# Lightning attention and a routed mixture of experts: rows of twelve attention steps turned on VectorE and written in groups of four, six steps with 128-key scores

## The chip, the cores and the metric

The kernel runs on one core of one Trainium2 chip. The time is device microseconds of one execution of the whole program; the result is compared as the median of several runs. Profiled executions are single executions, with their own time.

## The reference

The work has two parts, one feeding the other. First, linear attention with a decay: 4 sequences, 8 heads, 768 positions, head size 64, in float32.

```
for each block of positions:
    intra = (q_b @ k_b.T * lam**(i-j) for i >= j) @ v_b
    inter = (q_b * lam**(i+1)) @ kv_state
    out[block] = intra + inter
    kv_state = lam**block * kv_state + (k_b * lam**(block-1-j)).T @ v_b
x = out with the heads side by side      # 3072 tokens of 512 numbers
```

Then each token goes to one of 8 experts. The gate is `argmax(x @ w_gate)`, unless a local gate (`x @ w_local`) says that the token keeps the expert of the token before it in its sequence. The output of a token is its chosen expert's probability times `relu(x @ w1[e]) @ w2[e]`, with 1024 hidden units. All of it is float32.

## The kernel before

**Attention.** A chunk is 128 positions of one sequence; there are 24 steps `s`, ordered by chunk and within it by sequence (`ORDER`, so s%4 is the sequence b and s//4 the chunk c). One DMA brings the queries, keys and values of a step into a tile `inp` (1 MB, 0.75 MB in the last chunk); six such tiles exist (`LOADS`), so the load of step s+5 (`loaded`, L170) waits until step s-1 has done with its tile. GpSimd prepares three steps ahead: `qd` (L177, queries times powers of lambda) and `kd` (L180, keys times powers). Then, for a step:

- `scores` (L200 or L208): keys by queries into two PSUM tiles `ps`. A step in `WIDE` takes 128 keys at once, 8 matmuls of 128x128 (L200). Another takes 16 matmuls of 64 keys, where half of them skip the queries that lie before their keys (L208). VectorE multiplies the result by the decay mask into `sm` (L212). The same two PSUM tiles serve every step but step 1.
- `from_state` (L235): `qd` by the running state `kv` into `po`; ScalarE then scales the state (L239).
- `mix` (L248): values by `sm`, added in `po`; ScalarE copies it into `xc` (L251), features by tokens, one place for each sequence.
- `update` (L262): `kd` by values into `pk`, which VectorE adds to `kv` (L265; L267 in the first chunk).
- `rows_of(s-1)` (L272): four TensorE transposes of `xc` against the identity into PSUM, a ScalarE copy to `xn` (L277), and a DMA that writes the 128 token rows to `x_dram` (L281). The DMA is issued from ScalarE's queue, for the last steps from SyncE's (SP).

After each chunk, `gates` (L286) computes the gate sums of the four sequences and `logits` (L294, L295) turns them, at the next two steps. The table `extras` places the routing work (constants, the choice of experts, ranks, tables of tokens) at steps 6 to 22 on VectorE mostly: `constants_2` to `constants_6` hold casts of iota tables and of the identity matrix into other types (L333 to L353), `fresh_experts` is L389 to L403, `along_sequences` L411 to L420, `experts_of` L427 to L429, `ranks` L438 to L457.

**Order.** The attention loop writes out the order of the instructions for TensorE, VectorE, SyncE and GpSimd by hand; ScalarE's order is left to the scheduler. From step 5 on, the scores of step s+1 are issued at the start of step s; in steps 1 to 4 they follow `mix(s)`.

**Experts.** The tokens are gathered from `x_dram` by indirect DMA into tiles of 128 rows (L703), turned (L712, or VectorE's 32x32 transpose L717 with ScalarE copies L724), multiplied by the expert's weights (L731 and L737 for one tile at a time, L956 and L961 for two), scaled, and scattered to the output (L746). The weights lie in buffers `w1t` and `w2t` (2 MB each, two of each and a third from the expert stage on). Expert 0 is loaded at steps 16 to 20, expert 1 into `w1t[1]` and `w2t[1]` at the last step. Until then `w1t[1]` is unused, and `w2t[1]` holds start-up tables.

Of the kernel before, what the change touches and what calls it, by code (L numbers as in the profile page):

```python
# [8 lines left out]
F32 = mybir.dt.float32  # L9
# [14 lines left out]
P = 128  # L24
B, H, S, DH = 4, 8, 768, 64
A = H // 2
DM = H * DH
E, F = 8, 1024
DT, FT = DM // P, F // P
N = B * S  # L30
NT = N // P
NC = S // P
# [6 lines left out]
PARTS = [(0, 8), (8, NA), (NA, NT)]  # L39
LOADS = 6  # L40
QUARTERS = [16, 17, 18, 19]
WIDE = [3, 4, 5]
WARM = 10
KA = -(-(NA * P - E * (P - 1)) // P)

# [2 lines left out]
HP = P // 2  # L48
QP = P // 4
# [5 lines left out]
G = G2 + E  # L55
# [9 lines left out]
def kernel(  # L65
# [9 lines left out]
    nc = tc.nc  # L75
# [7 lines left out]
    x_dram = dram.tile([N, DM], F32, name="x_dram")  # L83
# [5 lines left out]
    w1t = [wts.tile([P, DT, F], F32, name=f"w1_{i}") for i in range(2)]  # L89
# [12 lines left out]
    ident = const.tile([P, P], F32, name="ident")  # L102
# [6 lines left out]
    load = x_ctx.enter_context(tc.tile_pool(name="load", bufs=LOADS))  # L109
# [54 lines left out]
    xc = att.tile([P, A, B, P], F32, name="xc", bufs=1)  # L164
    inp, qds, kds, sms, lgs = {}, {}, {}, {}, {}
# [103 lines left out]
    def rows_of(s):  # L269
        px = pg.tile([P, DM], F32, name="pk1")  # L270
        for a in range(A):
            nc.tensor.transpose(px[:, P * a:P * a + P], xc[:, a, ORDER[s][0]], ident)  # L272
        if s + 1 < NS:
            xn = att.tile([P, DM], F32, name="xn", bufs=4)
        else:
            xn = xlast
        nc.scalar.copy(xn, px)  # L277


        queue = nc.scalar if s + 3 < NS else nc.sync  # L280
        queue.dma_start(out=x_dram[P * s:P * s + P, :], in_=xn)  # L281

    def gates(k):

# [18 lines left out]
    count = const.tile([P, G + 1], F32, name="count")  # L303
    countb = const.tile([P, P], BF16, name="countb")
    whole = const.tile([P, G + 1], F32, name="whole")
# [24 lines left out]
            nc.gpsimd.memset(t[:, :, 0:1], 0.0)  # L330

    def constants_2():
        nc.vector.tensor_copy(count, ints[0][:, :G + 1])  # L333
        nc.vector.tensor_copy(whole, ints[0][:, P:P + G + 1])
        nc.vector.tensor_copy(identb, ident)
        nc.vector.tensor_scalar(down, count[:, :E], -1.0, float(E), ALU.mult, ALU.add)

    def constants_3():
        nc.vector.tensor_copy(countb, ints[0][:, :P])

    def constants_4():
        nc.vector.tensor_copy(beforeb, ints[1][:, P:2 * P].bitcast(F32))
        nc.vector.tensor_copy(parts[:, :, 0], whole[:, 1:NT + 1])
        nc.vector.tensor_copy(parts[:, :, 1], ints[0][:, 2 * P:2 * P + NT])

    def constants_5():
        for half in range(2):
            nc.vector.tensor_copy(dupb[:, HP * half:HP * half + HP], ident[:, :HP])
        nc.vector.tensor_reduce(upper, ident[:, HP:], axis=AX.X, op=ALU.add)

    def constants_6():
        for k in range(4):
            nc.vector.tensor_copy(dupq[:, QP * k:QP * k + QP], ident[:, :QP])  # L353
        row = ints[0][:, 2 * P:2 * P + 1]
        nc.vector.tensor_scalar(row, row, P - QP, None, ALU.bitwise_and)
        nc.vector.tensor_scalar(fourth, row, 1.0 / QP, None, ALU.mult)
# [424 lines left out]
    def extra_work(s, k):  # L781
        if (s, k) in extras:
            extras[s, k]()

    with tc.manual_schedule(engines={PE, DVE, SP, POOL}):

        warm = pg.tile([P, A, P], F32, name="pk0")
        for _ in range(WARM):
            nc.tensor.matmul(warm[:, 0], lhsT=ident, rhs=ident, start=True, stop=True)
        masks_of_lam()  # L790
        nc.gpsimd.memset(wgt, 0.0)
        constants_1()

        for s in range(LOADS - 1):
            inp[s] = load.tile([P, 4, DM], F32, name="inp")
        for s, half in ((0, 0), (1, 0), (0, 1), (1, 1), *((s, half) for s in range(2, LOADS - 1) for half in range(2))):
            nc.sync.dma_start(out=inp[s][:, 2 * half:2 * half + 2], in_=qkv[s][:, 2 * half:2 * half + 2])
        for s in range(3):
            prepare(s)
        scores(0)  # L800
        nc.sync.dma_start(out=wgt[:, :, :E + 1], in_=wg)
        for s in range(NS):
            if s + LOADS - 1 < NS:
                loaded(s + LOADS - 1)
            if s + 3 < NS and s != 1:
                prepare(s + 3)
            if s in QUARTERS:
                j = QUARTERS.index(s)
                nc.sync.dma_start(out=w1t[0][:, j], in_=w1_src(0)[:, j])
            if s == NS - 4:  # L810
                nc.sync.dma_start(out=w2t[0], in_=w2_src(0))
                weights(0)
            if s == NS - 1:
                nc.sync.dma_start(out=w1t[1], in_=w1_src(1))
                nc.sync.dma_start(out=w2t[1], in_=w2_src(1))
            if s + 1 < NS and s not in (1, 2, 3, 4, 5):
                scores(s + 1)
            from_state(s)
            if s % B == 1 and s > B:
                logits(s // B - 1)  # L820
            if s == 5:
                scores(6)
            extra_work(s, 0)
            if s % B == 0 and s:
                gates(s // B - 1)
            mix(s)
            if s == 0:
                update(0)
                query_powers(0)
            if s in (1, 2, 3, 4):  # L830
                scores(s + 1)
            if s == 1:
                query_powers(1)
                prepare(4)
                rows_of(0)
            if s:
                update(s)
            if s + 1 == NS:
                first_turned()
            if s > 1:  # L840
                rows_of(s - 1)
            extra_work(s, 1)
        x_ctx.close()
        act = ctx.enter_context(tc.tile_pool(name="act", bufs=2))
        w1t.append(act.tile([P, DT, F], F32, name="w1_2", bufs=1))
        w2t.append(act.tile([P, FT, DM], F32, name="w2_2", bufs=1))
        pools.append(act)

        pys.extend(pg.tile([P, DM], F32, name=f"pk{i}") for i in range(2))
        hq.update({(f, 1): act.tile([P, FT // 2, P], F32, name=f"h{f}1", bufs=1) for f in range(2)})  # L850
        xgh = act.tile([P, DM], F32, name="xgh", bufs=1)
        yt = act.tile([P, 2, DM], F32, name="y", bufs=1)
        xps = [act.tile([P, DT, P], F32, name=f"xp{i}", bufs=1) for i in range(3)]
        xs = act.tile([P, 3, DT // 2, P], F32, name="xs", bufs=1)
        s1 = act.tile([P, 3, DT // 2, F // 2], F32, name="s1", bufs=1)
        yl = s1[:, 0]
        s2 = act.tile([P, 3, FT // 2, DM // 2], F32, name="s2", bufs=1)
        hs = act.tile([P, 4, FT // 2, P], F32, name="hsum", bufs=1)
        part = act.tile([P, 3, FT // 2, P], F32, name="part", bufs=1)
        rest = act.tile([P, DM // 2], F32, name="rest", bufs=1)  # L860

        def finished(g):
            output(g % 2, g % 2)
            written(g, g % 2)

        def hiddens(g):
            hidden(g % 2, g % 2, 0)
            hidden(g % 2, g % 2, 1)


        xqs.extend((xlast, rt.tile([P, DM], F32, name="lg")))
        ahead(2, 0)
        xq = hq[1, 0].rearrange("p f i -> p (f i)")
        flipped(xq, xgt[1])
        ahead(3, 1)
        moved(xtt[1], xq, (0, 1))
        hidden(0, 0, 0)
        rows_of(NS - 1)
        weights(1)
        gates(NC - 1)  # L880
        moved(xtt[1], xq, (2, 3))
        hidden(0, 0, 1)
        by_slots(0, (2, 3, 4))
        logits(NC - 1)
        fresh_experts(2)
        flipped(xqs[1], xgt[0])
        ahead(4, 0)
        moved(xtt[0], xqs[1])
        finished(0)
        weights(2)  # L890
        along_sequences(2)
        flipped(xqs[0], xgt[1])
        hiddens(1)
        moved(xtt[1], xqs[0])
        experts_of(2)
        chances(2)
        flipped(xqs[1], xgt[0])
        finished(1)
        weights(3)
        ranks(2)  # L900
        masks(2)
        other_tiles()
        tokens_to_other_tiles()
        hiddens(2)
        moved(xtt[0], xqs[1])
        output(0, 0)
        weights(4)
        brought(1, (0, 1, 2, 3, 4))
        written(2, 0)
        hiddens(3)  # L910
        weights_of(KA, w_of(0), (1,))
        output(1, 1, range(FT // 2))
        by_slots(1, (0, 1, 2, 3, 4))
        output(1, 1, range(FT // 2, FT))
        written(3, 1)
# [417 lines left out]
```

## Time and profile before

| | us |
|---|---|
| median of 3 runs | 448.44 (448.04 to 448.66) |
| profiled execution, its own time | 449.21 |
| span of the profiled execution | 447.5 |
| TensorE matmul busy | 433.0 (97% of the span) |
| VectorE busy | 278.4 (62%) |
| ScalarE busy | 202.0 (45%) |
| GpSimd busy | 109.2 (24%) |
| mean granted TensorE clock | 0.995 |

In the profile, PE is TensorE, PEld its weight loads, DVE VectorE, ACT ScalarE, POOL GpSimd and SP SyncE; a q behind a name (SPq) means that the engine's queue issued something or waited. A busy TensorE in the table includes the pipelined ends of matmuls, so 97% does not mean peak. The attention stage fills the first 103 us or so of the span; the rest is the expert stage. A line of the page's groups reads: source line, engine, operation, output<-input, shapes, count | busy time, mean ns of one | idle time of the engine just before, and what ended it. A line of the chain of waits reads: start, length, and what held the end of the program back in that time. A line of the timeline reads: start, length, engine, line, operation, shapes, count, and in brackets how long the engine stood idle before it and what released it.

### The profile page before, as it was taken

How to read it: one execution, taken by the hardware profiler on the slowest of the kernel's cores; microseconds unless marked ns; L12 is line 12 of the kernel's file. 1: busy time of each engine (PE TensorE's matmuls, PEld its weight loads, DVE VectorE, ACT ScalarE, POOL GpSimd, SP SyncE). 2: the span in 40 equal slices, each digit the busy share in tenths (PEclk: the TensorE clock that was granted, in tenths of full speed). 3: DMA queues.
4: the chain of work that ended last, by engine and by line, in shares of the span. 5: the costliest groups of instructions: out<-in, count | busy, mean ns of one | idle time of the engine just before them, and what ended most of it. 6: DMA issues, size and time to landing. Idle time of an engine off the chain costs nothing.

```text
span 447.5 us, 10529 instructions
## 1 busy us (share of the span) xinstructions
PE 433.0 (97%) x4202; PEld 359.3 (80%) x4202; DVE 278.4 (62%) x562; ACT 202.0 (45%) x594; POOL 109.2 (24%) x120
## 2 busy tenths in 40 slices
PE   7999999999999999999999999999999999999993
PEld 6877877768667866979686999667899999898982
DVE  5546867881419949866473796100487888878661
ACT  2355656546453205553434447451445455556110
POOL 4476656231100041204120301210102011020101
PEclk9999999999999999999999999999999999999997
DMA  8999989988899889999995699997153838380101
GB/s 267 409 420 392 323 305 320 354 305 325 275 403 365 325 277 378 398 395 404 394 399 214 180 403 372 346 368 254 41 212 107 313 97 287 140 280 4 53 3 51
DMA packets 42575, 124.85 MB, mean 279 GB/s; under 512 B 3148, under 2 KB 3148, under 8 KB 40592
## 3 DMA queue, kind: packets, MB, share of 16 engines
q1 hardware_dynamic: 34976, 104.62, 64.0%
q0 software_dynamic: 4368, 13.90, 8.8%
q10 hardware_dynamic: 3168, 5.51, 3.3%
q8 instruction: 37, 0.61, 0.5%
q14 instruction: 26, 0.21, 0.1%
HBM read 124.02 MB, written 12.91 MB: 306 GB/s over the span
## 4 chain that ended last, share of the span: by engine, by line
PE 82%; DMA 7%; issue 6%; DVE 3%; POOLq 0%; POOL 0%
PE ps L731 13%; PE pk L737 12%; PE ps L956 12%; PE pk L961 11%; DMA out_dram<-y,sidxp 6%; PE po L248 6%; PE po L956 5%; PE pl L961 4%; PE ps L208 4%; PE pk L272 3%; PE po L235 2%; PE pk L262 2%; PE pr L1117 2%; PE pr L1095 2%; PE pl L286 1%
## 5 line engine op out<-in xcount | busy, mean ns | idle before, releaser
L731 PEld LDWEIGHTS ps<-xt,w 128*128 128x128 f32 x512 | 58.2, 192 | 3.0 <-issue 2.3
L731 PE MATMUL ps<-xt,w 128*128 128x128 f32 x512 | 59.1, 276 | 0.3 <-DVE xt L713 0.3
L737 PE MATMUL pk<-w,h 128*128 128x512 f32 x128 | 56.5, 593 | 0.0
L737 PEld LDWEIGHTS pk<-w,h 128*128 128x128 f32 x128 | 23.6, 190 | 26.3 <-issue 25.6
L746 POOL DMA_INDIRECT out_dram<-y,sidx x14 | 14.0, 1002 | 105.8 <-DVE y L763 46.5
L212 DVE TENSOR_TENSOR sm<-ps,mask 128x512 f32<-128x512 f32 x46 | 29.6, 685 | 16.1 <-PE ps L208 6.6
L703 POOL DMA_INDIRECT xg<-x_dram,gidx x25 | 25.8, 1032 | 55.2 <-DVE lg L717 24.6
L724 ACT COPY xp<-xlast 32x128 f32<-32x128 f32 x128 | 37.8, 295 | 1.7
L733 ACT ACTIVATE h<-ps 128x512 f32<-128x512 f32 x16 | 9.6, 597 | 57.6 <-PE ps L731 57.6
L724 ACT COPY xp<-lg 32x128 f32<-32x128 f32 x112 | 33.0, 295 | 2.6
L763 DVE TENSOR_SCALAR y<-pk,gate 128x512 f32<-128x512 f32 x8 | 6.0, 745 | 42.1 <-PE pk L737 40.0
L956 PEld LDWEIGHTS ps<-xp,w 128*128 128x128 f32 x256 | 30.5, 192 | 1.7 <-issue 1.3
L177 POOL TENSOR_TENSOR qd<-inp,lamq 128x512 f32<-128x512 f32 x20 | 25.6, 1278 | 25.1 <-PE po L235 15.8
L956 PE MATMUL ps<-xp,w 128*128 128x128 f32 x256 | 31.3, 275 | 0.0
L956 PE MATMUL ps<-xs,s 128*128 128x128 f32 x256 | 31.2, 275 | 0.0
L248 PE MATMUL po<-sm,inp 128*64 128x128 f32 x384 | 28.1, 280 | 2.5 <-DVE sm L212 1.4
L961 PE MATMUL pk<-w,h 128*128 128x256 f32 x128 | 30.5, 381 | 0.0
L961 PE MATMUL pk<-s,hsum 128*128 128x256 f32 x128 | 30.3, 380 | 0.0
L956 PEld LDWEIGHTS ps<-xs,s 128*128 128x128 f32 x256 | 29.9, 192 | 0.0
L248 PEld LDWEIGHTS po<-sm,inp 128*64 128x64 f32 x384 | 21.3, 136 | 10.2 <-issue 7.7
L961 PEld LDWEIGHTS pk<-s,hsum 128*128 128x128 f32 x128 | 23.9, 190 | 3.3 <-DVE s L1044 0.2
L961 PEld LDWEIGHTS pk<-w,h 128*128 128x128 f32 x128 | 23.5, 190 | 3.4 <-issue 0.6
(280 smaller groups left out, 793.9 us busy)
## 6 DMA issues: line engine op xcount, KB each, us to landing
w<-in_w_dram SPq DMA_DIRECT2D x43, 2048.0 KB, 11.8
inp<-in_qkv_dram SPq DMA_DIRECT2D x15, 1024.0 KB, 8.8
x_dram<-xn ACTq DMA_DIRECT2D x21, 256.0 KB, 7.4
inp<-in_qkv_dram SPq DMA_DIRECT2D x10, 512.0 KB, 7.9
inp<-in_qkv_dram SPq DMA_DIRECT2D x4, 768.0 KB, 6.9
w<-in_w_dram SPq DMA_DIRECT2D x4, 512.0 KB, 9.3
x_dram<-xn SPq DMA_DIRECT2D x2, 256.0 KB, 8.6
xg<-x_dram,gidx POOLq DMA_INDIRECT x25, 6.3
```

Of the source, the lines that this page charges most:

```text
L177: nc.gpsimd.tensor_tensor(qd, x[:, 0].rearrange("p (a i) -> p a i", i=P), lamq, ALU.mult)
L208: nc.tensor.matmul(ps[u][half, a, first:], lhsT=kt[rows, a, half], rhs=qt[rows, a, first:], start=True, stop=True, skip_group_check=True)
L212: nc.vector.tensor_tensor(sm[:, u], ps[u], mask[:, u], ALU.mult)
L248: nc.tensor.matmul(head(a, u), lhsT=vn[:, a, u], rhs=sm[:, u, a], start=(not c and a < 2), stop=True, skip_group_check=True)
L272: nc.tensor.transpose(px[:, P * a:P * a + P], xc[:, a, ORDER[s][0]], ident)
L703: nc.gpsimd.indirect_dma_start(out=xg, out_offset=None, in_=x_dram[:n, :], in_offset=bass.IndirectOffsetOnAxis(ap=gidx[i][:, j:j + 1], axi ...
L724: copy(xt[QP * j:QP * j + QP, :, QP * k:QP * k + QP], blocks[QP * k:QP * k + QP, :, j])
L731: nc.tensor.matmul(ph[:, j], lhsT=w1t[w][:, d, P * f:P * f + P], rhs=xtt[i][:, d], start=(d == 0), stop=(d == DT - 1))
L737: nc.tensor.matmul(pys[i], lhsT=hq[f // 4, i][:, f % 4], rhs=w2t[w][:, f], start=(f == 0), stop=(f == FT - 1))
L746: apart(nc.gpsimd.indirect_dma_start(out=out, out_offset=bass.IndirectOffsetOnAxis(ap=sidx[i][:, j:j + 1], axis=0), in_=y, in_offset=None, ...
L956: nc.tensor.matmul(to[:, m], lhsT=a[:, k, P * m:P * m + P], rhs=b[:, k], start=(new and not m and not k), stop=(k == 1), skip_group_check= ...
L961: nc.tensor.matmul(to, lhsT=a[:, f], rhs=b[:, f], start=(new and not f), stop=(f == FT // 2 - 1), skip_group_check=True)
```

## The change

- For rows 0 to 11 `rows_of` is no longer called. Instead `turned_rows(r)` runs at the end of step r+1 (`TURNED`; row 11 at step 13): one VectorE transpose of 32x32 blocks from `xc` into a quarter of a 1 MB area in `w1t[1]`.
- After rows 3, 7 and 11 (at the ends of steps 4, 8 and 13) `group_out` issues four DMAs on SyncE's queue. Each writes the 32 partitions of one block row, for four steps: 512 pieces of 512 bytes, 256 KB.
- The blocks leave the features of a row in another order. The other rows get the same order from their ScalarE copy (L277), and the host array of `w1` is permuted to it.
- `WIDE` gains steps 7, 9 and 11.
- The thirteen casts of `constants_2` to `constants_6` move from VectorE to ScalarE.

```diff
--- before.py
+++ after.py
@@ -39,7 +39,8 @@
 PARTS = [(0, 8), (8, NA), (NA, NT)]
 LOADS = 6
 QUARTERS = [16, 17, 18, 19]
-WIDE = [3, 4, 5]
+WIDE = [3, 4, 5, 7, 9, 11]
+TURNED = {**{r: r + 1 for r in range(3 * B)}, 11: 13}
 WARM = 10
 KA = -(-(NA * P - E * (P - 1)) // P)
 
@@ -274,11 +275,32 @@
             xn = att.tile([P, DM], F32, name="xn", bufs=4)
         else:
             xn = xlast
-        nc.scalar.copy(xn, px)
+        nc.scalar.copy(xn.rearrange("p (j d c) -> p j d c", j=4, c=QP), px.rearrange("p (d j c) -> p j d c", j=4, c=QP))
 
 
         queue = nc.scalar if s + 3 < NS else nc.sync
         queue.dma_start(out=x_dram[P * s:P * s + P, :], in_=xn)
+
+    groups = {}
+
+    def turned_rows(s):
+
+        k = s // B
+        if k not in groups:
+            xn = w1t[1].rearrange("p t f -> p (t f)")[:, B * DM * (k % 2):B * DM * (k % 2) + B * DM]
+            if k + 1 == NC:
+                xn = load.tile([P, 4, DM], F32, name="inp").rearrange("p n m -> p (n m)")
+            groups[k] = xn.rearrange("p (b i m) -> p b i m", b=B, i=4)
+        nc.vector.transpose(groups[k][:, s % B].rearrange("p i (d c) -> p i d c", c=QP),
+                            xc[:, :, s % B].rearrange("p d (i c) -> p i d c", c=QP))
+
+    def group_out(k):
+
+        n = sum(r // B == k for r in TURNED)
+        rows = x_dram[B * P * k:B * P * k + n * P, :]
+        for j in range(4):
+            nc.sync.dma_start(out=rows[:, P * j:P * j + P].rearrange("(i a) m -> a i m", a=QP),
+                              in_=groups[k][QP * j:QP * j + QP, :n].rearrange("a b i m -> a (b i) m"))
 
     def gates(k):
 
@@ -330,27 +352,27 @@
             nc.gpsimd.memset(t[:, :, 0:1], 0.0)
 
     def constants_2():
-        nc.vector.tensor_copy(count, ints[0][:, :G + 1])
-        nc.vector.tensor_copy(whole, ints[0][:, P:P + G + 1])
-        nc.vector.tensor_copy(identb, ident)
+        nc.scalar.copy(count, ints[0][:, :G + 1])
+        nc.scalar.copy(whole, ints[0][:, P:P + G + 1])
+        nc.scalar.copy(identb, ident)
         nc.vector.tensor_scalar(down, count[:, :E], -1.0, float(E), ALU.mult, ALU.add)
 
     def constants_3():
-        nc.vector.tensor_copy(countb, ints[0][:, :P])
+        nc.scalar.copy(countb, ints[0][:, :P])
 
     def constants_4():
-        nc.vector.tensor_copy(beforeb, ints[1][:, P:2 * P].bitcast(F32))
-        nc.vector.tensor_copy(parts[:, :, 0], whole[:, 1:NT + 1])
-        nc.vector.tensor_copy(parts[:, :, 1], ints[0][:, 2 * P:2 * P + NT])
+        nc.scalar.copy(beforeb, ints[1][:, P:2 * P].bitcast(F32))
+        nc.scalar.copy(parts[:, :, 0], whole[:, 1:NT + 1])
+        nc.scalar.copy(parts[:, :, 1], ints[0][:, 2 * P:2 * P + NT])
 
     def constants_5():
         for half in range(2):
-            nc.vector.tensor_copy(dupb[:, HP * half:HP * half + HP], ident[:, :HP])
+            nc.scalar.copy(dupb[:, HP * half:HP * half + HP], ident[:, :HP])
         nc.vector.tensor_reduce(upper, ident[:, HP:], axis=AX.X, op=ALU.add)
 
     def constants_6():
         for k in range(4):
-            nc.vector.tensor_copy(dupq[:, QP * k:QP * k + QP], ident[:, :QP])
+            nc.scalar.copy(dupq[:, QP * k:QP * k + QP], ident[:, :QP])
         row = ints[0][:, 2 * P:2 * P + 1]
         nc.vector.tensor_scalar(row, row, P - QP, None, ALU.bitwise_and)
         nc.vector.tensor_scalar(fourth, row, 1.0 / QP, None, ALU.mult)
@@ -832,13 +854,16 @@
             if s == 1:
                 query_powers(1)
                 prepare(4)
-                rows_of(0)
             if s:
                 update(s)
             if s + 1 == NS:
                 first_turned()
-            if s > 1:
+            if s > 1 and s - 1 not in TURNED:
                 rows_of(s - 1)
+            for r in [r for r in TURNED if TURNED[r] == s]:
+                turned_rows(r)
+                if r + 1 not in TURNED or r % B == B - 1:
+                    group_out(r // B)
             extra_work(s, 1)
         x_ctx.close()
         act = ctx.enter_context(tc.tile_pool(name="act", bufs=2))
@@ -1318,7 +1343,7 @@
         "qkv": _np.stack([packed[b, c] for b, c in ORDER]),
         "lam": i["lam"],
         "wg": swapped(_np.concatenate([i["moe_w_gate"], i["moe_w_local"]], 1)).reshape(DT, P, E + 1).transpose(1, 0, 2),
-        "w1": swapped(i["moe_w1"]),
+        "w1": swapped(i["moe_w1"]).reshape(E, DT, 4, QP, F).swapaxes(1, 2).reshape(E, DM, F),
         "w2": i["moe_w2"],
     }
     arrays = {f"in_{n}_dram": _np.ascontiguousarray(a) for n, a in arrays.items()}
```

## Prediction

> **What bounds the kernel now.** I read the page's busy shares first, then the chain of waits over the attention stage, then the table by stretches and the timeline there.
>
> ```profile
> PE 433.0 (97%) x4202; PEld 359.3 (80%) x4202; DVE 278.4 (62%) x562; ACT 202.0 (45%) x594; POOL 109.2 (24%) x120
> ...
> DMA  8999989988899889999995699997153838380101
> ```
>
> TensorE is busy nearly throughout, so time is gained only where its queue gets shorter or stops waiting. The DMA digits are 8 and 9 over the attention stage too (the first nine slices, 11.2 us each): a second resource without much room. The chain over one ordinary step, s=8:
>
> ```profile
> 39.15 0.81 PE ps L208 x24
> 39.96 0.45 PE po L235 x16
> 40.41 0.99 PE pl L286 x8
> 41.41 1.02 PE po L248 x16
> 42.43 0.47 PE pk L262 x16
> 42.90 0.59 PE pk L272 x4
> 43.48 0.81 PE ps L208 x24
> ```
>
> Columns: start, length, what held the end back. All links are TensorE's: scores, state product, gates (every fourth step), mix, update, and 0.59 us for the four transposes of L272. So a regular step is 0.81+0.45+1.02+0.47+0.59 = 3.34 us, and L272 stands on the path. Not everywhere, though. From the timeline, step 2 to 3:
>
> ```profile
> 17.02 1.29 DVE L212 TENSOR_TENSOR sm<-ps,mask 128x512 f32<-128x512 f32 x2 [1.35 <-PE ps L200]
> 17.53 0.42 PEld L272 LDWEIGHTS pk<-ident,xc 128*128 128x128 f32 x4
> 17.53 0.66 PE L272 MATMUL pk<-ident,xc 128*128 128x128 f32 x4
> ...
> 18.11 1.33 PE L248 MATMUL po<-sm,inp 128*64 128x128 f32 x16
> ```
>
> Here L248 needs the mask product that ends at 18.31, and takes 1.33 instead of the later 1.09: TensorE meets VectorE, and the transposes fill a wait. From step 3 on state products or a score queued a step ahead separate the two.
>
> Loads, from the answer on line L170 and the table of stretches (columns: length, PE, PEld, DVE, ACT, POOL busy, clock, DMA share, GB/s):
>
> ```profile
> DMA to landing us min/median/max: 6.9/8.4/12.5
> 23.50:42.90 19.40, 18.52 (x397) 14.97 (x394) 10.93 (x20) 11.02 (x33) 13.64 (x12) 1.00 1.02 415
> 42.90:63.00 20.10, 19.19 (x420) 15.38 (x422) 15.40 (x46) 11.72 (x38) 11.25 (x10) 1.00 0.96 326
> ```
>
> DMA is full until about 43 us, then as busy at a lower rate. VectorE has 0.56 of the first stretch and 0.77 of the second.
>
> [...]
>
> **The change, part by part.**
>
> TensorE, removed: twelve groups of L272 (rows 0 to 11), 12 x 0.59 = 7.1 us. Rows 0 and 1 fall where the mask product ends last: mask end 14.75 and 18.31 hold L248, whose ends then move by about 0.1 each. That takes back 2 x 0.49 = 1.0. Left: 6.1.
>
> TensorE, added: steps 7, 9 and 11 become wide. The chain has the wide scores (L200) at 1.09 us, the narrow at 0.81 with a tail that overlaps L235. I take 0.33 us more a step, 3 x 0.33 = 1.0; nothing if VectorE is what the step waits for, 0.43 if the overlap goes too. Left: 5.1.
>
> VectorE: twelve transposes, by the row
>
> ```profile
> L717 DVE STREAM_TRANSPOSE lg<-xg 128x512 f32<-128x512 f32 x4 | 2.8, 695 | 0.0
> ```
>
> add 8.3 us. Input is read in runs of 32 here; I keep 0.695 and allow up to twice that. The thirteen casts that leave (L333 0.86, L334 0.17, L335 1.07, L339 0.82, L342 0.82, L343/344 0.4, L348 0.8, L353 1.0) take off 5.9. Net +2.4. The transpose stands after the state add and before the next mask product. An ordinary step of VectorE is 0.42+0.70+1.29 = 2.4 us, TensorE's new step 3.34-0.59 = 2.75: it fits. The next scores reuse the same PSUM, so they wait for that mask product: update end +0.2 +0.42 +0.65 +1.29 = 2.6 against 2.75. Routing at s=9 to 11 adds 1 to 1.6 us a step (L295, L399 to L403, L414 0.40, L420 0.67), and there VectorE is late by about 1.0 us in all; before, those four steps took 15.94 us (43.48 to 59.42) against 15.24 of TensorE work, 0.7 of it waits already. Net 0.3 lost. Left: 4.8.
>
> ScalarE: loses twelve copies of 0.59 and twelve DMA issues of 0.33; gains thirteen small casts at the start, by the built order between L150 (ends 7.5) and the first xc copy:
>
> ```profile
> 10.99 0.65 ACT L251 COPY xc<-po 128x256 f32<-128x256 f32 x2 [3.50 <-PE po L248]
> ```
>
> It was idle for 3.50 us before it. At 0.2 to 0.28 each (64x4 copies took 0.2, queued 128x64 ones 0.265) they need 2.6 to 3.6: hidden in that idle time, at worst 0.2 late. POOL finished their source (L320 to L324) at 3.1. The permuted copy of the other rows keeps its size; bound -0.1 to +0.1 each, off the path. The permutation of w1 is on the host.
>
> SP and DMA: three groups of four writes, 1.05 MB each, enter SP's queue at the ends of steps 4, 8 and 13, each waiting for VectorE's transpose. Behind it stand loads 10, 14 and 19, held by about 1.3 us of wait and 4 x 0.35 of issue. Who needs them: the scores four steps later. The timeline has kd of step 4 released by its load at 16.42; at 420 GB/s a 1.05 MB load takes 2.5 us, and ACT's writes no longer mix in. With g for a group, loads 10, 14, 19 land at 31.4+g, 41.4+2g, 53.9+3g. They are needed at about 40.4, 54.6 and 75.9 (before's 43.48, 59.42 and 80.70 less what is gained by then). [...] Cost taken: nothing. Low end g=2.8 (queue q10 moved 5.51 MB in 3.3% of 447.5 us, 2.7 us a MB); high end 11.2, if four times as many packets each took as long. POOL sees its loads later, but works three steps ahead. The first half of w1t[1] is written again at s=8's row, long after its first group has left; its expert load comes at s=23.
>
> Expert stage: its loads and gathers are issued relative to the steps, its chain is TensorE's throughout, so it starts earlier by the same amount. No DMA wait stands there to be uncovered.
>
> Sum: 7.1-1.0-1.0-0.3 = 4.8 us. The profiled execution ran 449.21 us (span 447.5) against the median of 448.44: it becomes 444.4 (span 442.7), and the median 443.6.
>
> **Rivals.**
>
> *All of it counts*: wide scores lie in VectorE's shadow, no wait appears: 7.1 gained, 441.3. For it: VectorE's 2.6 nearly equals a step. Against: step 2's waits.
>
> *VectorE becomes the bound*: the strided transpose takes 1.39 us. An ordinary narrow step is then 3.1 against 2.75, four of them lose 0.36 each, the two worst routing steps 0.7 each, 2.8 in all: 446.4. [...]
>
> *The 512-byte writes become the bound, slower*: SP's ring holds loads behind the groups, scores wait for inp. Loss is the larger of 2g-13.2 and 3g-22; it eats 4.8 at g = 9 us, 117 GB/s. At g=10 it loses 8: 451.6. For it: packets four times as many,[...] and a DMA that after 43 us is busy 0.96 at only 326 GB/s. Against: no wait of TensorE for a load is seen now, with 8.4 us landing against some 14 of need.
>
> *No change*: part of the gain is lost to a wait not seen here (TensorE stops without a named cause, such as 0.88 at 36.78): 448.4.
>
> **How the numbers follow.** Main case 0.60 (own range 442.0 to 445.3), all counts 0.10, VectorE 0.14, no change 0.05, DMA 0.11. The likeliest is 443.6. A measurement of this kernel tells about 0.2%, 0.9 us. The range 440.9 to 447.5 leaves out the last two cases and a little at the low end. Faster 0.84, same 0.05, slower 0.11.
>
> **What would show it.** L272 falls from 96 matmuls to 48; steps 5 to 12 take about 0.5 us less each; the last row transposes start near 102 instead of 107; ACT's first xc copy stays at 11 us. Wrong if the strided transpose is well over 0.7 us, if SP's group takes over 7 us to land, or if scores wait for inp.

## The result, and the profile after

After took 446.49 us (median of 20 runs, 444.1 to 449.75) where before took 449.32 in the same session: ratio 0.9937, 95% interval 0.9916 to 0.9957, so 2.8 us less where 4.8 were forecast. A second measurement of the same kernel gave 0.9925 (0.9895 to 0.9955), 3.4 us. The profiled execution ran 447.07 us, its span 445.3, at a mean clock of 0.992. The page:

```profile
PE 429.3 (96%) x4106; PEld 356.6 (80%) x4106; DVE 285.8 (64%) x561; ACT 196.9 (44%) x595; POOL 109.4 (25%) x120
...
DMA  7999999989899889999994799996164838370101
```

TensorE has 96 matmuls fewer (48 transposes, 48 of the scores) and is busy 3.7 us less; VectorE has 7.4 us more. The DMA row is full over the attention stage as before. The chain of waits over step 8:

```profile
34.53 1.09 PE ps L201 x16
35.63 0.60 PE po L236 x16
36.22 0.99 PE pl L308 x8
37.22 1.02 PE po L249 x16
38.24 0.47 PE pk L263 x16
38.71 0.81 PE ps L209 x24
```

The transposes are gone and nothing waits in their place. The scores queued here (for step 9) are wide. The step takes 4.18 us; before it took 4.33 with narrow ones. The timeline between steps 2 and 3:

```profile
16.63 1.29 DVE L213 TENSOR_TENSOR sm<-ps,mask 128x512 f32<-128x512 f32 x2 [0.73 <-PE ps L201]
...
17.43 1.64 PE L249 MATMUL po<-sm,inp 128*64 128x128 f32 x16 [0.21 <-issue]
...
18.17 0.70 DVE L294 STREAM_TRANSPOSE w<-xc 128x512 f32<-128x512 f32 x1
```

The mix starts before the mask product ends (17.92) and is stretched to 1.64 us, so the early rows gain little, as forecast (0.31 us by step 3). The transpose fits behind the mask; all twelve, from the groups by form:

```profile
L294 DVE STREAM_TRANSPOSE w<-xc 128x512 f32<-128x512 f32 x12 | 8.4, 700 | 0.0
```

700 ns with the strided input, against the 695 assumed. The loads (the answer on L171) and the two stretches of the prediction:

```profile
DMA to landing us min/median/max: 6.5/10.4/13.1
```

```profile
23.50:42.90 19.40, 19.40 (x432) 16.51 (x431) 14.72 (x31) 9.60 (x33) 12.94 (x12) 1.00 0.99 371
42.90:63.00 20.10, 16.88 (x393) 13.70 (x391) 17.68 (x41) 9.80 (x35) 13.89 (x13) 1.00 0.98 359
```

In the first stretch TensorE has no gap at all (18.52 of 19.40 before), in the second it loses 3.22 us (0.91 before). A load lands 10.4 us after its issue in the middle, two more than before. The chain shows what stands in the second stretch:

```profile
46.94 0.13 PE pr L449 x2
47.07 1.48 issue
48.55 1.09 PE po L249 x16
...
54.02 0.36 PE ps L209 x3
54.38 0.74 issue
55.12 0.73 PE ps L209 x23
...
59.93 0.32 PE po L236 x9
60.25 0.99 issue
61.24 0.45 PE po L236 x7
```

"issue" here is TensorE standing with no released wait to name, twice amid a row of equal matmuls. What such a pause has in common is seen in the DMA view. Of its stretch 46.0 to 47.2 us (columns: packets, MB, share of 16 engines):

```profile
q1 hardware_dynamic: 727, 0.39, 107.8%
q8 instruction: 1, 0.02, 5.6%
```

A packet of 16 KB on the queue for instructions travels among 727 others. By the records it ends at 47.15, and TensorE goes on 1.40 us later. The same holds for all seventeen pauses over 0.6 us without a named releaser in before, after and the profiles of e8, e9, e13 and e14 below: each ends 1.2 to 1.6 us behind such a packet, of which one comes about every 6 us. In all twenty profiles there are 47 such pauses, and the distance is 1.19 to 1.61 us in every one. So these records suggest that TensorE waits for instructions there; most packets bring no pause.

The lead over before, by the start of each step's mix, counted from the first mix of the same execution:

| step | after | e13: no group writes | e14: before without 12 row writes |
|---|---|---|---|
| 4 | 0.59 | 0.59 | -0.16 |
| 7 | 2.33 | 2.33 | 0.25 |
| 10 | 4.56 | 3.87 | 0.13 |
| 13 | 5.11 | 6.67 | 1.88 |
| 16 | 3.96 | 6.83 | 2.03 |
| 19 | 4.23 | 6.83 | 2.31 |
| 20 | 2.20 | 7.31 | 2.31 |
| 23 | 2.14 | 6.28 | 1.92 |

From step 4 to 7 each step gains 0.58, as forecast. After's lead falls at its pauses and rises at those of before (36.78 and 60.45 us). Over the attention stage the pauses behind a packet add up to 3.2 us in before and to 3.2 in after, so in this pair they cancel. With the pauses of both taken out, after leads by 5.1 us at step 19 and by 2.2 at step 23: 2.9 us are lost between steps 19 and 20. In the second profile of after (e8) the pauses add up to 6.1 us, in e13 to 1.4; with the pauses taken out, these two lead by 4.6 and 4.5 us at step 23. So the forecast 4.8 us are there but for two losses, the stretch from step 19 to 20 in after and longer pauses in e8. This is an estimate from single executions. The span's gain (2.2) is about the lead at the end of the attention stage, so the expert stage passed it through.

### The profile page after: what moved, and what is told of

Read it like the earlier page. It is cut to its first block, busy times and chain, and to the rows that moved or that the text cites. A ratio compares the mean times of both kernels' runs of the same rounds, so it can differ in the third digit from the quotient of the medians.

```text
span 445.3 us, 10363 instructions
## 1 busy us (share of the span) xinstructions
PE 429.3 (96%) x4106; PEld 356.6 (80%) x4106; DVE 285.8 (64%) x561; ACT 196.9 (44%) x595; POOL 109.4 (25%) x120
## 4 chain that ended last, share of the span: by engine, by line
PE 82%; DMA 6%; issue 6%; DVE 3%; POOL 0%; POOLq 0%; ACT 0%
PE ps L753 13%; PE pk L759 12%; PE ps L981 12%; PE pk L986 11%; DMA out_dram<-y,sidxp 6%; PE po L249 5%; PE po L981 5%; PE pl L986 4%; PE ps L209 3%; PE po L236 2%; PE pr L1142 2%; PE pr L1120 2%; PE pk L263 2%; PE pl L308 2%; PE ps L201 1%
## 6 DMA issues: line engine op xcount, KB each, us to landing
inp<-in_qkv_dram SPq DMA_DIRECT2D x15, 1024.0 KB, 10.4
```

## The experiments

All were timed in five rounds beside before, e1 to e4, e5 to e8, e9 to e12, e13 to e16 and e17, e18 each on one chip.

| | median us (runs) | ratio to before | 95% interval |
|---|---|---|---|
| e7 before, six wide | 447.18 (8) | 0.9941 | 0.9910 to 0.9972 |
| e3 after, three wide | 448.97 (22) | 0.9978 | 0.9956 to 1.0000 |
| e5 after, eleven wide | 446.29 (13) | 0.9932 | 0.9907 to 0.9958 |
| e8 after again | 446.72 (7) | 0.9925 | 0.9895 to 0.9955 |
| e1 quarters late | 446.34 (10) | 0.9916 | 0.9888 to 0.9945 |
| e6 groups behind load | 446.36 (15) | 0.9921 | 0.9894 to 0.9948 |
| e2 groups on ACT | 456.31 (6) | 1.0140 | 1.0094 to 1.0186 |
| e4 2 KB pieces | 449.79 (14) | 0.9970 | 0.9936 to 1.0004 |
| e9, e10 before, shifted | 450.96, 451.35 (14, 22) | 1.0001, 1.0008 | 0.9979 to 1.0032 |
| e11 after, shifted | 449.03 (22) | 0.9963 | 0.9942 to 0.9984 |
| e12 after, shifted more | 450.69 (22) | 1.0000 | 0.9975 to 1.0025 |
| e13 after, no group writes | 443.53 (6) | 0.9853 | 0.9820 to 0.9885 |
| e14 before, no row writes | 448.75 (22) | 0.9959 | 0.9943 to 0.9975 |
| e15 after, no turns | 447.17 (6) | 0.9923 | 0.9896 to 0.9950 |
| e16 after, neither | 444.96 (6) | 0.9893 | 0.9858 to 0.9928 |
| e17 rows singly | 452.79 (22) | 1.0039 | 1.0018 to 1.0060 |
| e18 no writes, three wide | 444.28 (6) | 0.9848 | 0.9812 to 0.9883 |

**SP's queue.** The first theory was that SP stood. The waits of SP's queue in after (columns: us in total, times, longest; L317 stands just behind a transpose on VectorE):

```profile
SPq L171 <- PE pk L263: 13.1, 6, 3.5
SPq L302 <- DVE w L294: 12.0, 2, 7.0
SPq L831 <- DMA x_dram<-xn: 11.8, 3, 8.2
...
SPq L302 <- DVE lt L317: 5.7, 1, 5.7
```

The three groups wait 17.7 us in all for VectorE's transposes (12.0 and 5.7), and the quarter load of an expert's weights (L831) 11.8 us for a ScalarE row write. Loads stand behind both. Four kernels change that.

e1, the quarters all at step 19:

```
-            if s in QUARTERS:
-                j = QUARTERS.index(s)
-                nc.sync.dma_start(out=w1t[0][:, j], in_=w1_src(0)[:, j])
+            if s == QUARTERS[-1]:
+                for j in range(4):
+                    nc.sync.dma_start(out=w1t[0][:, j], in_=w1_src(0)[:, j])
```

> The changed kernel, but the four quarter loads of expert 0's first weights are all issued at step 19, after the last attention load, where the changed kernel issues them at steps 16 to 19. Theory A (SyncE's queue stands still at the first quarter load, which waits 8.2 us for a row write of ScalarE; the loads of steps 22 and 23 come 5 us late, GpSimd's qd with them[...]): the loads go out on time, the pause of 1.44 us before L641 goes and the clock stays at 1.0 there; ratio to the kernel before about 0.989 (the changed kernel has 0.9937). Rival B (the lost time is instruction fetches of TensorE and a clock drop that fall where they fall): no change from 0.9937 within 0.001.

As after. A load of L171 now stood for the row write in the place of the quarter, 10.9 us in one wait.

e2, the groups on ScalarE's queue:

```
-            nc.sync.dma_start(out=rows[:, P * j:P * j + P]...
+            nc.scalar.dma_start(out=rows[:, P * j:P * j + P]...
```

> The changed kernel with the twelve group writes issued from ScalarE's queue instead of SyncE's. Theory A: loads 10, 14 and 19 are issued some 4 to 6 us earlier (they stand no longer behind 3.4 to 6.0 us of write issues), GpSimd waits less for loads, ratio 0.991 or lower, if the issues do not hold up ScalarE's copies of xc; if each group stands 3 to 6 us in ScalarE's queue as it did in SyncE's, TensorE waits for xc and po and the ratio is 0.998 or above. Rival B: 0.9937.

Slower than before by 6.3 us. Its chain through the first group:

```profile
27.52 0.50 ACTq L302
...
28.06 0.50 ACTq L302
...
28.60 5.45 ACTq L302
```

Issuing one of the DMAs held ScalarE for 5.45 us, with the copy of `xc` behind it; TensorE stood 4.61 us here, 2.64 and 1.96 at the other groups, and the granted clock was half for 6.8 us from 31.9 us on and for 3.4 us from 52.4 and from 76.3 us on.

e4, one DMA for a group, from 128 partitions in pieces of 2 KB:

```
-        for j in range(4):
-            nc.sync.dma_start(out=rows[:, P * j:P * j + P].rearrange("(i a) m -> a i m", a=QP),
-                              in_=groups[k][QP * j:QP * j + QP, :n].rearrange("a b i m -> a (b i) m"))
+        nc.sync.dma_start(out=rows.rearrange("(p b) m -> p b m", b=n),
+                          in_=groups[k][:, :n].rearrange("p b i m -> p b (i m)"))
```

> The changed kernel, but each group is written by one DMA from 128 partitions in pieces of 2 KB; the rows of tokens 0 to 1535 land in a wrong arrangement, so the expert outputs are those of other numbers, with the same routing and the same amount of work. Theory A: one issue instead of four and whole-width pieces, loads 10, 14 and 19 go out within 2 us of their buffers' release, GpSimd's waits for loads fall from 15 us to under 6, ratio 0.990. Rival B: 0.9937. If the 512-byte pieces themselves are the cost, a group takes about 2.8 us here against 4.8 to landing before, and the ratio falls with it by up to 0.004 more.

Not better than after over all fourteen runs, but they lie far apart: 442.64 and 443.77, then twelve from 447.00 to 452.54. The issue of a DMA took 0.33 us here. The profile is of the fastest run: its lead over before is 6.0 us at step 23, and TensorE waits for VectorE no more than in before. So one execution wrote all groups and had the whole gain, while most did not. Whether the 512-byte pieces or the four issues cost what is missing in after stays open.

e6, each group issued a step later, behind that step's load, and the quarters as in e1:

```
             if s + LOADS - 1 < NS:
                 loaded(s + LOADS - 1)
+            if due:
+                group_out(due.pop())
...
-                    group_out(r // B)
+                    due.append(r // B)
```

> The changed kernel with each group of writes issued one step later, behind that step's attention load instead of ahead of it, and the four quarter loads all at step 19. Theory A (loads behind the groups come late, GpSimd late with them[...]): loads 10, 14 and 19 go out when their buffers come free, GpSimd waits under 8 us for loads in all (15 us in the changed kernel, 25 in e1), ratio 0.989. If the loads are late because of the DMA engines themselves and not of the queue's order: waits as before, ratio 0.9937.

Within the interval of after, though SP's wait for transposes fell from 17.7 to 3.7 us and loads 10, 14 and 19 were issued at 25.3, 39.3 and 57.8 us instead of 30.6, 46.1 and 65.0. Other loads came late in their place (load 15 at 46.9, load 20 at 68.1), and one stood 8.2 us for a row write. SP's wait for the transposes alone is not the cause.

**Rows and wide steps one at a time.** e3 is after with `WIDE = [3, 4, 5]`, e5 after with steps 13, 15, 17, 19 and 21 wide as well, e7 before with nothing but `WIDE = [3, 4, 5, 7, 9, 11]`, e8 after unchanged, beside e5 to e7.

> The changed kernel with WIDE back at steps 3, 4 and 5. My prediction's term (a wide step costs TensorE 0.33 us on the path): 1.0 us faster than the changed kernel, ratio 0.9915. Rival (at steps 7, 9 and 11 VectorE is the later one, so the wide scores lie in its shadow): same, 0.9937. Second rival (more instructions of TensorE to fetch, one more fetch pause): 0.9955.

> The changed kernel with five more wide steps (13, 15, 17, 19, 21), eleven in all. Theory C (TensorE's pauses are fetches of its own instructions, which end some 1.4 us after a 16 KB instruction packet lands behind a full DMA; a wide step has 8 matmuls fewer to fetch; e3 lost about 1.8 us by 3 narrow steps): fewer and shorter pauses, 1 to 3 us faster than the changed kernel, ratio 0.988 to 0.991. My prediction's term (0.33 us of TensorE work for each wide step): 1.7 us slower, ratio 0.9975. Theory of VectorE's shadow (only steps 7, 9 and 11 have VectorE later than TensorE): the same 0.9975.

> The kernel before with WIDE at the six steps, nothing else of the change. Theory C (fewer TensorE instructions to fetch): faster than before by 0.5 to 2 us, ratio 0.996 to 0.999. My prediction's term: 1.0 us slower, ratio 1.002.

> The changed kernel itself, for a comparison on the same chip as the three others and a second profile of it. All theories: ratio 0.9937 within its interval. Theory A: the stretch 76 to 90 us shows again a pause of TensorE behind a VectorE instruction that stood beside a GpSimd one; theory C: pauses that end 1.3 to 1.6 us after an instruction packet, 3 to 5 us of them in the stage.

The turned rows alone (e3) brought 1.0 us instead of 5.8. The wide steps, priced at plus 1.0, brought 2.6 in before (e7) and about 2 in after (e3 against after). Both terms of the sum were off, in opposite directions. Five wide steps more changed nothing. The chain of e7 over step 8:

```profile
38.83 1.09 PE ps L200 x16
39.92 0.60 PE po L235 x16
40.52 1.00 PE pl L286 x8
41.52 1.02 PE po L248 x16
42.54 0.47 PE pk L262 x16
43.00 0.59 PE pk L272 x4
43.59 0.81 PE ps L208 x24
```

4.76 us against 4.33 in before: here the wide scores cost 0.43, the upper end of the price. The gain came elsewhere. By the records e7's TensorE paused 1.2 us behind packets of instructions between 9 and 104 us, before 3.2, e5 not at all. (In e5 it waited 3.7 us for VectorE instead.) A wide step has 32 fewer TensorE instructions (matmuls and weight loads). Both e7 and before have 37 such packets, though, so it isn't that a packet less is read, and e3 with 4.4 us lies between the two profiles of after. That wide steps gain by shorter pauses is indicated by one execution of each, no more; how is open.

**Where the packets fall.** Perhaps such pauses come by chance of where a packet ends in the program. e9 to e12 put small multiplications ahead of the first input (twenty in e9 and e11, thirty-six in e10 and e12):

```
-WARM = 10
+WARM = 6
...
+        for _ in range(20):
+            nc.tensor.matmul(warm[:QP, 0, :2], lhsT=ident[:, :QP], rhs=ident[:, :2], start=True, stop=True)
```

> Before, with four full warming multiplications fewer and twenty tiny ones more ahead of the first input: 64 TensorE records more, all of it before the data comes, so no work on the path changes. The page counts 37 packets of the instruction queue for 8404 matmul and load records, one for 227, so the place where a packet ends in the program moves by 0.28 of a packet in every step. If the pauses of TensorE that end 1.3 to 1.6 us behind such a packet are what swings the result (three of 0.84 to 0.88 us in the profile of before), they stand elsewhere and the time moves by about 1 to 3 us from that of before, either way. If the time is set by work and waits for data alone: 450 us, within 0.2% of before.

> The same with thirty-six tiny multiplications: 128 records more, 0.56 of a packet. Instruction theory: the pauses stand elsewhere again and the time differs from before and from the quarter shift by 1 to 3 us. Theory of work and data alone: within 0.2% of before, perhaps up to 0.3 us more for the longer start.

> After, with the same shift of 64 records. Instruction theory: the pauses of the profiled after (1.48, 0.74, 0.99 us) move, and the time lies 1 to 3 us from that of after, either way; the mean over the shifts of after against the mean over those of before then tells what the change is worth by itself. Theory of work and data: 446.5 us, within 0.2% of after. My sum of the prediction, if the shifts average the pauses out: after's three placings lie 4.8 us under before's three on the mean.

> After, shifted by 128 records. Instruction theory: 1 to 3 us from after, either way. Theory of work and data: within 0.2% of after.

The pauses did move: to 41.77, 64.39 and 82.96 in e9, where before has 36.78, 60.45 and 90.04. Their sums stayed near each other (before 3.2, e9 3.8, e10 4.6). But the small multiplications took 55 ns a pass, and the first mixes came later by about 1.6 us in e11 and 3.3 in e12. By their ratios they lie 1.2 to 1.7 and 2.8 to 3.4 us behind after, which this delay explains. So the test was spoiled as a measure of placing; before took such a delay without loss (e9, e10), which stays unexplained.

**Taking the suspects out.** These four and e18 gather the expert stage's rows from the input:

```
-        nc.gpsimd.indirect_dma_start(out=xg, out_offset=None, in_=x_dram[:n, :],
+        nc.gpsimd.indirect_dma_start(out=xg, out_offset=None, in_=rows_in[:n, :],
```

e13 leaves out the group writes, e15 the transposes, e16 both:

```
                 turned_rows(r)                                     # not in e15, e16
-                if r + 1 not in TURNED or r % B == B - 1:          # e13, e16
-                    group_out(r // B)
...
-                              in_=groups[k][QP * j:QP * j + QP, :n]...    # e15
+                              in_=ident[QP * j:QP * j + QP].unsqueeze(1).to_broadcast([QP, 4 * n, P]))
```

e14 is before with `if s >= 3 * B:` ahead of the row write, e18 is e13 with `WIDE = [3, 4, 5]`.

> After without the twelve DMAs of the groups; so that no unwritten row is read, the expert stage gathers its rows from the input instead (rows of other values, the same transfers). The transposes stay. Theory of the writes (the groups' waits and slow issues on SP make loads late, and the late loads cost the rest of the gain): the 0.6 us of each turned row arrive, 443.5 to 445 on a chip on which before takes 450, and 5 us under e14. Theory of VectorE (the transposes lengthen the chains of the gates and of the last steps): 446 to 447, as after. Theory of instruction fetch (TensorE that runs faster only pauses longer): as after too.

> The counterpart in before: ScalarE's row writes of the first twelve steps left out, TensorE's transposes and ScalarE's copies kept, the expert stage gathers from the input as in e13. It tells what the write traffic by itself costs. In before the writes go by another queue than the loads and no wait of the chain names them: 450, within 1 us of before. If the transfers themselves slow the instruction packets and the loads: 1 to 3 us less.

> After with the group writes, in the same pieces and places of SP's queue, but from the identity instead of a turned buffer, and with the twelve VectorE transposes left out (the expert stage gathers from the input). SP no longer waits for VectorE, but issues as much. VectorE theory: 5 us or more under before, 444 to 445. Theory of the writes, if it is their issue and traffic: as after, 446 to 447; if it is SP's wait for the transposes: 444 to 445 too, which e13 against e16 then tells from VectorE. Fetch theory: as after.

> After with neither transposes nor group writes: the twelve rows are not turned or written at all (the expert stage gathers from the input). This is the most that taking 12 x 0.59 us from TensorE can bring. Writes theory or VectorE theory: 443 to 444.5, 5.5 to 7 us under before. Fetch theory: no better than after by more than 1 us, because neither removed work was on the path.

> e13 (after without group writes, gather from the input) with WIDE = [3, 4, 5]. The price of the three wide steps without the group writes around them. My sum: 3 x 0.33 = 1.0 us less than e13. If wide steps gain by themselves, as e7 against before and after against e3 have it: 2 us more than e13. If turned rows alone bring the whole without the writes, e18 lies 5.5 to 6 under e14.

Without group writes the missing time is there: e13 lies 4.8 us under e14 (0.0106 of 450.7, give or take 1.7), where 4.8 were forecast. e16 lies 3.0 us under it and e18 5.0, as uncertain; by the same sum they should have brought 5.1 and 5.8. Taking the transposes away brings nothing that can be seen, with writes (e15, as after) or without (e16 against e13). So the transposes are not the cause, and the writes are. The new source of the expert stage's rows is not either, for e15 has it too and runs as after. Against e13 the groups cost after 3.5 us, against the mean of e13 and e16 2.6; the row writes that they replace cost before 1.8 (give or take 0.7). One pair is weaker: e16 lies only 1.4 us under e15, give or take 2.0. The clearest is e18 under e3, both with three wide steps: 5.9, give or take 1.9.

Where it shows: GpSimd's waits for loads in before, in after and in e13:

```profile
POOL qd L177 <- DMA inp<-in_qkv_dram: 2.0, 3, 0.8
```

```profile
POOL qd L178 <- DMA inp<-in_qkv_dram: 8.7, 9, 2.5
```

```profile
POOL qd L178 <- DMA inp<-in_qkv_dram: 1.0, 4, 0.3
```

(Its waits for loads on `kd` all lie in the first 20 us.) The load of step 19 lands at 62.5 us in e13 and at 73.7 in after. Of after's pauses the one at 47.07 stands while group packets are under way (by the records, 1775 of 512 bytes from 44 to 48 us), and e13 has none over 0.6 us between 30 and 75 us. Three sums over the attention stage, in us, one execution of each:

| | TensorE's pauses behind packets | GpSimd's waits for loads after 20 us | TensorE's waits for VectorE, 20 to 95 us |
|---|---|---|---|
| before | 3.2 | 2.0 | 0.3 |
| e14: before, no row writes | 2.1 | 2.4 | 0.3 |
| after, e8 | 3.2, 6.1 | 8.7, 13.1 | 2.2, 0.7 |
| e15: after, no turns | 3.6 | 18.8 | 1.8 |
| e13, e16: no group writes | 1.4, 2.2 | 0.7, 0.8 | 0.3, 0.3 |
| e18: no writes, three wide | 3.2 | 0.6 | 0.0 |

The second and third columns go with the group writes on SP's queue, and e15 shows them without any transpose; in e2, where ScalarE issues the groups, GpSimd waits only 0.4 us. The pauses do so less clearly: they are 3.2 us in before, in the first after and in e18 alike. How the third column can follow from the second is seen in the timeline of after:

```profile
83.58 1.26 POOL L178 TENSOR_TENSOR qd<-inp,lamq 128x512 f32<-128x512 f32 x1 [2.49 <-DMA inp<-in_qkv_dram]
83.61 1.44 DVE L631 TENSOR_TENSOR val<-hit,parts 128x60 bf16<-128x60 bf16 x2
```

The late product on GpSimd stands exactly beside a small VectorE operation, which then takes as long as it; in e13 the two of L631, from the answer on `val`, took

```profile
L631 DVE TENSOR_TENSOR val<-hit,parts x2: 218/223/228, 80.4 to 80.6; 128x60 bf16<-128x60 bf16 x2
```

TensorE waits for `val` from 83.67 to 85.11. The longer of the two took 1.31 us, against 0.22 in e13 and in before. What ties it to the product on GpSimd the traces do not show. Then, from 86.4 us, the granted clock is half for 3.413 us, which makes the gate sums 1.86 us instead of 0.99. TensorE had stood for 1.44 and 0.26 us just before (to 85.11 and 85.71 us); what set the half clock off stays open. In the second profile of after the late product met the operation before `val` instead: it took 1.20 us (0.21 in the first), `val` 0.36 for both, and TensorE waited 0.40. The clock did not fall, but TensorE paused 1.19 and 0.96 us at 73.03 and 80.08. So the loss takes different roads in different executions.

The wide steps' price looks different here too: e18, with three of them, is 0.2 us faster than e13, its counterpart with six (give or take 2.2), and 1.1 faster than the mean of e13 and e16. That fits the price of plus 1.0, and fits no price just as well; a gain of 2 lies at the edge. So the gain of wide steps was seen only beside writes: there, six in place of three bring 2 us.

**Singly.** e17 is e6 with each row written by itself, 48 DMAs instead of 12:

```
-                group_out(due.pop())
+                row_out(due.pop())
...
-                if r + 1 not in TURNED or r % B == B - 1:
-                    due.append(r // B)
+                due.append(r)
```

> As e6 (writes one step behind the transposes, behind that step's load, the quarter loads together at step 19), but each turned row is written by itself: four DMAs of 64 KB in every step in place of four of 256 KB in every fourth. The whole traffic and the 512-byte pieces stay. If it is the burst of 1 MB ahead of a load that costs what e13 gets back: 2 to 3 us less than e6 and after, 443.5 to 444.5 on a chip on which before takes 450. If it is the traffic itself, or SP's time to issue: as e6, 446 to 447, or more, since 48 DMAs are issued instead of 12.

5.3 us slower than e6 by the ratios. Its waits:

```profile
POOL qd L178 <- DMA inp<-in_qkv_dram: 31.6, 14, 6.1
...
PE ps L209 <- DMA inp<-in_qkv_dram: 9.0, 6, 4.7
```

The scores themselves wait for loads, the prediction's slow rival, by another road: SP reaches each load late (the load of step 16 is issued at 57.7 us, at 49.1 in e6). Late in the longest of these waits the granted clock falls to half, for 6.8 us. With 48 issues in place of 12 the kernel tells nothing of the burst by itself. No kernel here is clearly faster than after with all its work done; e1 and e6 are within its interval.

## Why the prediction was wrong

- **TensorE removed, 12 x 0.59 less 1.0.** Right. L272's count fell to 48, each step from 4 to 7 gained 0.58, and where no writes disturb, e13 gained the 4.8 of the sum (e16 and e18 3.0 and 5.0, where 5.1 and 5.8 were due).
- **Wide steps, plus 1.0.** Right on the path (0.43 at step 8 of e7); e18 can't tell it from nothing. Wrong in the kernel as it is: minus 2.6 in before, minus 2 in after. The step took the work alone; what is seen beside it are shorter pauses (1.2 us in e7, 3.2 in before), and how they come about is open.
- **VectorE, 0.3 lost.** Right that the transposes are not the bound: 700 ns each, and e15 shows nothing to be had.
- **ScalarE's casts.** Hidden: its first copy of `xc` began at 10.61 us (10.99 before), after an idle 2.16.
- **SP and DMA, "Cost taken: nothing".** This is the step that failed: the groups cost 2.6 to 3.5 us (5.9 with three wide steps) and save 1.8 of row writes. It asked only whether a load lands before the scores need it, and there it was right: in after no scores wait for a load, and a group's packets travel for 5.6 to 6.3 us (28.9 to 34.5 us for the first), though among loads, within the range of 2.8 to 11.2. Where in that range g would lie was an estimate that no run had shown, and with 11.2 load 10 would have landed at 42.6 us, 2.2 late. (The 420 GB/s taken for a load is near what before moved from 20 to 40 us, 419.) But others wait for the same DMA. "POOL works three steps ahead" was no cover: GpSimd's waits for loads grew from 2.0 to 8.7 us, its late products met VectorE's routing work, and TensorE waited 2.2 us for VectorE where before waits 0.3 (0.7 in e8, which had 2.9 us more of pauses instead). The queue time was too small as well: loads 10, 14 and 19 were issued 5.3, 6.8 and 7.2 us later than in e6, where they stand ahead of the groups; 2.7 had been taken (1.3 of wait and four issues of 0.35, where an issue took up to 2.79).
- **Expert stage, nothing lost.** Right. The last row transposes moved only from 106.95 to 104.43 us, not to 102.
- **The rivals.** "No change" had a hint, TensorE's stops without a named cause, but as a chance of 0.05 and without their cause; before has as many of them as the first profile of after. The bound by 512-byte writes would have shown as scores that wait for loads, and after has none; what the pieces cost is open (e4). VectorE's rival named 446.4, which is what was measured, but by luck: its cause was a transpose of 1.39 us, and it took 0.70.
- **Luck.** That 2.8 us arrived at all is in part two errors that offset each other: the turned rows alone brought 1.0 where 5.8 were due (e3), and the wide steps brought a gain of 2 where a loss of 1.0 was.

Open is what in the groups' traffic costs most: later issue (e6), larger pieces (e4) and smaller bursts (e17) each changed something else too, and none regained it but for two runs of e4. One theory less: SP's wait for the transposes (e15 has none and runs as after).

## What to carry to other kernels

Where the DMA row of the page is full, a write moved to the queue of the loads is not free because the scores' loads still come in time: ask who else waits for those loads, and what a late engine will meet. Read "issue" pauses amid equal matmuls beside the instruction queue, and add them up in both profiles, before counting removed TensorE work as gain. To find a lost gain, leave out each new thing by itself, and its old counterpart in the kernel before.

## What the runs showed of the hardware

- TensorE's pauses without a releaser, 0.65 to 2.29 us, each ended 1.2 to 1.6 us behind a 16 KB packet of the instruction queue (47 in twenty profiles).
- A VectorE product of 128x60 took 1.31 us (after), 1.29 (e5) and 1.20 (e8) beside a GpSimd product of about as long, and 0.21 to 0.23 otherwise.
- Half-clock windows of 3.4 or 6.8 us came with stops of TensorE of 1.4 to 4.7 us in after, e2 and e17; pauses of 1.8 to 2.3 us in e8, e1, e4 and e3 brought none.
- A DMA of 512 pieces of 512 bytes can hold its issuer. The first of a group took 0.33 us in after, those behind it up to 2.79: the answer on L302 in after, and in e2 from ScalarE (ns, least/median/most).

```profile
L302 SPq DMA_DIRECT2D x_dram<-w x12: 326/748/2791, 26.8 to 63.5; - x12
```

```profile
L302 ACTq DMA_DIRECT2D x_dram<-w x12: 314/594/5452, 27.1 to 71.3; - x12
```

- With 128 partitions and pieces of 2 KB the same group took 327 ns to issue and 7.7 us to land (e4); of the four DMAs in after the one with a known landing took 4.8.
